# Score products by one Strassen step per pair of token tiles, with two x buffers refilled by GpSimd, in an FNet + PEER kernel

## The chip, the cores and the metric

The kernel runs on one core of one Trainium2 chip. The metric is the device time of one execution in microseconds, as the median of the runs. Before the change it is 764.75 us in three runs (764.59, 764.75 and 765.51).

## The reference

x has 2048 tokens of 640 values. Two branches are mixed by a gate of each token.

```python
# A: FNet.  y = Re(DFT_seq(DFT_hidden(x)))
a = einsum("bsd,ed->bse", x, dft_hid_re);  b = einsum("bsd,ed->bse", x, dft_hid_im)
y = einsum("ts,bse->bte", dft_seq_re, a) - einsum("ts,bse->bte", dft_seq_im, b)
# B: PEER. 32 heads, 2 x 16 keys of 128 values, 256 experts, the best 2 of each head
q = einsum("nd,dhc->nhc", x, w_q)
s1 = einsum("nhd,ed->nhe", q[..., :128], k1);  s2 = einsum("nhd,ed->nhe", q[..., 128:], k2)
# the best 2 of s1 and of s2, their 4 sums, the best 2 of these: top_s, top_e
g = softmax(top_s)
act = gelu(einsum("nd,nhkd->nhk", x, u[top_e]))
out = einsum("nhk,nhk,nhkd->nd", g, act, v[top_e])
gate = sigmoid((x * gate_w).sum(-1))
return gate * y + (1 - gate) * out
```

## The kernel before

All large products are made with operands split in two: a number is rounded to fp32r (h, on ScalarE), the rest l = f - h is taken by a second engine (`split`, L124), and `mm3` (L129) makes three matmuls: h·h, h·l and l·h.

The program goes through 128 **pieces** of the sequence DFT (`seq_piece`, L208). A piece is one of 2 DFT matrices (real, imaginary), 4 column chunks of 512 and 16 tiles of x; it has 15 matmuls of 128x512, which add into PSUM banks 0 to 4. Behind every 16th piece the five banks are copied to the tile ST, VectorE multiplies them by the gates (`gate_piece`), and `store_piece` stores the block P to DRAM (tile pd, five transfers of 256 KB). The x tiles X0 to X15 (h and l of 128x640 each) are made once and stay in SBUF. The DFT matrix comes in piece by piece: loaded by SP five pieces ahead (`load_piece`, tile wf), split three pieces ahead into one of four slots of WS (`split_piece`, L167: h by ScalarE, l by a GpSimd subtraction).

Other work is hung on the pieces by `at(n, f)`: f is emitted behind piece n.

- Pieces 0 to 29: the keys are folded into w_q (`w_part`, L333; w_q comes in 32 transfers of 640 KB, tile wq), which gives a matrix W of 640 x 1024 (32 heads x 2 x 16 keys) in WH and WL; `split_u` prepares u. x transposed comes in per pair of token tiles (`load_xT`, tile xf) and is split into xh and xl (`split_xT`, L370, the l part on GpSimd).
- Pieces 31 to 62: one pair of token tiles per 4 pieces. `score_half` (L429) makes the scores of one tile and one half of the columns, 15 matmuls of 128x512 behind a piece, in banks 5 and 6 by turns; ScalarE copies them to the tile sc. `u_pair` (L576) makes the products with all 256 experts' u for both tiles, 30 matmuls of 128x256 in the same banks, then gelu on ScalarE and two stores, issued by ScalarE.
- VectorE finds the best two of each head (`topk`, L444: maxima, eq, powers, tied) and, after every 4 tiles, the gates (`gates`, L478, with an exp on ScalarE, L500). Later one-hot tables (hot, `experts`) and their products (L668) turn the gates into sums per expert. The order of this work is set by a queue of generators, the **Pump** (L45): TensorE's emitted time gives credit (0.95 of it), and each operation gives back its assumed cost by `yield`. So the costs in the program set where VectorE's work stands among the rest; they are no measured times.
- From piece 128 on, the last stage: 84 steps of two Strassen products with the hidden DFT and v (`step`, L948). DD, the split hidden DFT matrix, is made in pieces from about 66 on (`split_dd`, L709, with GpSimd).

The dependencies between engines are found from the order of the program (semaphores are put in by it); each engine and each DMA queue works its own list in order.

Of the kernel before, what the change touches and what calls it, by code (L numbers as in the profile page):

```python
# [40 lines left out]
AHEAD = 5  # L41
BYPASS = 4

# [51 lines left out]
def gated_mix_kernel(ctx: ExitStack, tc: tile.TileContext, xT, xn, dreT, dimT, wsre, wsim, wq, kT, uT, vv, gw, out):  # L95
# [43 lines left out]
    gdr = dram.tile([2 * S], F32, name="gdr")  # L139
    bg = Pump()  # L140
# [14 lines left out]

    pieces = [(w, c, s) for w in range(2) for c in range(NC) for s in range(NT)]
# [43 lines left out]
    def store_piece(q):  # L200
# [4 lines left out]
        for d in range(KD):  # L205
            eng.dma_start(pd[w, c][d], staged.pop((q, d)))
# [21 lines left out]
    for q in range(2 * NC):  # L228
        n = NT * (q + 1)
        at(n + (2 if q == 0 else -2 if q > 1 else -1), load_row, q)  # L230
        at(n + (7 if q == 0 else 0), gate_piece, q)
        at(n + (8 if q == 0 else 1), store_piece, q)
# [42 lines left out]
    gwb = p1.tile([P, D], F32, name="gwb")  # L275
# [21 lines left out]
    io = p1.tile([P, P], F32)  # L297
# [50 lines left out]
    def split_w(G):  # L348
        c = slice(P * G, P * (G + 1))
        split(wp.pop(G), WH[:, :, c], WL[:, :, c], nc.vector)  # L350
# [3 lines left out]
    def load_u(k):  # L354
        uf[k] = p1.tile([P, NE], F32, name="uf", bufs=2)
        nc.sync.dma_start(uf[k], uT[k])
# [19 lines left out]

    for n in range(NT - 4):
        at(n, load_x, n + 4)
# [7 lines left out]
    for G in range(NG):  # L386
        b = 6 + 3 * G
        for m in range(4 * G, 4 * G + 4):
            at(b, w_part, m)
        at(b, split_w, G)  # L390
        for i, m in enumerate(range(4 * G + WQB, 4 * G + WQB + 4)):
            at(b + i // 2, load_wq, m)
# [7 lines left out]
    at(n - 2, load_xT, 1)  # L400
    N0 = n + 1
# [27 lines left out]
    def score_half(i, a):  # L429
        xh, xl = (xs[t][:, i % 2] for t in ("xh", "xl"))  # L430
        if a == 0:
            while i > 1 and i - 2 not in picked:
                bg.one()
            scs[i] = p2.tile([P, HH, E], F32, name="sc", bufs=2)
        ps = ps_s()
        c = slice(a * TC, (a + 1) * TC)
        for k in range(KD):
            mm3(ps, xh[:, k, :], xl[:, k, :], WH[:, k, c], WL[:, k, c], k == 0, k == KD - 1)
            run_bg(0.68)
        nc.scalar.activation(scs[i].rearrange("p h e -> p (h e)")[:, c], ps, AF.Copy)  # L440
        if a == 1:
            picks(i, scs.pop(i))

    def topk(i, sc):  # L444


        b, ib = divmod(i, NB)
        if ib == 0:
            stats[b] = [p2.tile([P, 2, NB, HH], F32, name=t) for t in ("mm", "tied")]
        mm, tied = stats[b]  # L450
        eq = p2.tile([P, HH, E], F16, name="eq", bufs=1)
        for s in range(2):
            m = mm[:, s, ib, :]
            nc.vector.tensor_reduce(m, sc, op=OP.max, axis=AX.X)  # L454
            yield 1.22
            nc.vector.tensor_tensor(eq, sc, m[:, :, None].to_broadcast([P, HH, E]), op=OP.is_equal)  # L456
            yield 1.31
            if s == 0:
                nc.vector.scalar_tensor_tensor(sc, eq, FAR, sc, op0=OP.mult, op1=OP.add)
                yield 1.44  # L460
            nc.vector.tensor_tensor(eq, eq, powers[:, None, :].to_broadcast([P, HH, E]), op=OP.mult)
            yield 1.0
            nc.vector.tensor_reduce(tied[:, s, ib, :], eq, op=OP.add, axis=AX.X)  # L463
            yield 1.22
# [111 lines left out]
    def u_pair(p):  # L576
        xh, xl = xs["xh"], xs["xl"]
        ps = ps_s((P, 2, 2 * P))
        for n in range(2):
            c = slice(n * P, (n + 1) * P)  # L580
            for k in range(KD):
                mm3(ps[:, n, :], UH[:, k, c], UL[:, k, c], xh[:, :, k, :], xl[:, :, k, :], k == 0, k == KD - 1)
            run_bg(1.8)
        act = p2.tile([P, 2, 2 * P], F32, name="act", bufs=2)
        nc.scalar.activation(act, ps, AF.Gelu_apprx_tanh)
        for n in range(2):
            nc.scalar.dma_start(actd[n][:, 2 * p * P:2 * (p + 1) * P], act[:, n])

    for p in range(NP):
        n = N0 + 4 * p  # L590
        for a in range(4):
            if a == 2:
                at(n + 3, u_pair, p)
                at(n + 3, split_xT, p + 1, 0)
            at(n + 1 + a, score_half, 2 * p + a // 2, a % 2)
        at(n + 4, split_xT, p + 1, 1)
        at(n + 6, load_xT, p + 2)
    N1 = N0 + 4 * NP + 1

# [13 lines left out]
    def experts():  # L613
# [33 lines left out]
        def build(g, c, s):  # L647
# [7 lines left out]
            for o, a, b, op in ((pt, row(0), wt, OP.is_equal), (qt, row(1), wt, OP.is_equal), (pt, pt, row(2), OP.mult)):  # L655
                nc.vector.tensor_tensor(o, a, b, op=op)  # L656
                yield 1.1 + settle()
# [62 lines left out]
    for m in range(KD):  # L720
        for a in range(2):
            at(N1 + 3 + 4 * m + 2 * a, split_dd, m, a)
        at(N1 + 7 + 4 * m, load_dd, m + 2)

# [386 lines left out]
```

## Time and profile before

| what | time |
|---|---|
| median of the runs | 764.75 us (764.59 to 765.51) |
| the profiled execution | 764.93 us |
| its span | 763.2 us |
| TensorE busy | 757.8 us (99%) |
| VectorE busy | 558.7 us (73%) |
| GpSimd busy | 342.6 us (45%) |
| ScalarE busy | 314.4 us (41%) |
| DMA moved | 130.34 MB, mean 171 GB/s |

The span is what the profiler saw of one execution, from its first to its last instruction; 764.93 - 763.2 = 1.7 us lie around it. Engines: PE is TensorE's matmuls, PEld its weight loads (beside the matmuls), DVE VectorE, ACT ScalarE, POOL GpSimd, SP the engine that only issues DMAs; ACTq, SPq are the lists that issue DMAs from an engine. Names such as `sc<-b` are output and input by the program's names, b a PSUM bank. Matmuls are pipelined, so the shown length of one is longer than the distance to the next. L numbers are lines of the program before; in the quoted rows of the changed program, of that one.

### The profile page before, as it was taken

The page shows a single profiled execution, that of the slowest core. Times are in us where ns is not written, and L with a number is a line of the kernel's source. Part 1 is how long each engine was busy: PE and PEld are TensorE (multiplying, and loading weights), DVE is VectorE, ACT ScalarE, POOL GpSimd, SP SyncE. Part 2 cuts the span into 40 slices and gives each one's busy share as a digit, 9 for nine tenths or more (in the row PEclk, how much of TensorE's full clock was granted, in tenths as well). Part 3 has the DMA queues.
Part 4 walks back from the last instruction along what each step waited for, and adds up shares of the span by engine and source line. Part 5 has one row for each costly group of instructions (what it writes and reads, how often), then busy time and mean ns, then how long its engine had stood idle before and what let it go on. Part 6 is the DMA issues. An engine that isn't in the chain of part 4 may idle for free.

```text
span 763.2 us, 11112 instructions
## 1 busy us (share of the span) xinstructions
PE 757.8 (99%) x4091; PEld 620.5 (81%) x4091; DVE 558.7 (73%) x653; ACT 314.4 (41%) x558; POOL 342.6 (45%) x254
## 2 busy tenths in 40 slices
PE   9999999999999999999999999999999999999998
PEld 7777777888888888888888888888888788888886
DVE  6863152566899699999699979669989995357651
ACT  4434123221224442623533784533544653543441
POOL 5533235142242323433148664444357694487252
PEclk9999999999999999999999999999999999999999
DMA  9988695321213322320535342568855659775301
GB/s 335 356 311 314 240 368 210 111 76 42 76 57 79 107 97 64 123 52 21 166 129 168 119 154 72 176 196 289 297 196 193 201 207 368 245 231 175 111 28 70
DMA packets 73398, 130.34 MB, mean 171 GB/s; under 512 B 14848, under 2 KB 22144, under 8 KB 73088
## 3 DMA queue, kind: packets, MB, share of 16 engines
q1 hardware_dynamic: 63040, 113.16, 44.7%
q10 hardware_dynamic: 10304, 16.47, 6.0%
q8 instruction: 32, 0.52, 0.3%
q14 instruction: 22, 0.18, 0.1%
HBM read 102.84 MB, written 25.18 MB: 168 GB/s over the span
## 4 chain that ended last, share of the span: by engine, by line
PE 97%; DVE 1%; POOL 1%; ACT 0%; issue 0%; POOLq 0%
PE b L131 31%; PE b L133 30%; PE b L132 30%; PE b L340 2%; PE b L218 2%; PE b L668 1%; PE b L286 0%; DVE hot L656 0%; DVE vxl L127 0%; POOL WS L127 0%; ACT b L626 0%; DVE tf L760 0%; POOL ts L127 0%; DVE ST L998 0%; ACT WS L126 0%
## 5 line engine op out<-in xcount | busy, mean ns | idle before, releaser
L127 POOL TENSOR_TENSOR WS<-wf,WS 128x512 fp32r<-128x512 f32 x127 | 191.6, 1512 | 254.9 <-ACT WS L126 243.9
L131 PE MATMUL b<-WS,X 128*128 128x512 f32 x620 | 243.2, 392 | 0.0
L132 PE MATMUL b<-WS,X 128*128 128x512 f32 x620 | 241.4, 389 | 0.0
L133 PE MATMUL b<-WS,X 128*128 128x512 f32 x620 | 241.3, 389 | 0.0
L131 PEld LDWEIGHTS b<-WS,X 128*128 128x128 f32 x620 | 116.4, 188 | 28.1 <-issue 3.6
L133 PEld LDWEIGHTS b<-WS,X 128*128 128x128 f32 x620 | 116.4, 188 | 24.3
L132 PEld LDWEIGHTS b<-WS,X 128*128 128x128 f32 x620 | 116.4, 188 | 23.7
L126 ACT ACTIVATE WS<-wf 128x512 fp32r<-128x512 f32 x127 | 79.7, 629 | 103.4 <-PE b L133 50.7
L656 DVE TENSOR_TENSOR hot<-rows,wtab 128x1024 f16<-128x1024 f16 x64 | 64.2, 1026 | 12.6 <-PE b L668 12.6
L454 DVE TENSOR_REDUCE mm<-sc 128x64 f32<-128x1024 f32 x32 | 38.8, 1212 | 41.2 <-ACT sc L440 41.2
L127 POOL TENSOR_TENSOR xl<-xf,xh 128x640 fp32r<-128x640 f32 x16 | 28.9, 1811 | 80.0 <-ACT xh L126 80.0
L440 ACT ACTIVATE sc<-b 128x512 f32<-128x512 f32 x32 | 19.8, 619 | 108.1 <-PE b L133 108.1
L131 PE MATMUL b<-WU,xh 128*128 128x512 f32 x160 | 62.3, 390 | 0.0
L132 PE MATMUL b<-WU,xh 128*128 128x512 f32 x160 | 62.3, 390 | 0.0
L133 PE MATMUL b<-WU,xl 128*128 128x512 f32 x160 | 62.2, 389 | 0.0
L127 POOL TENSOR_TENSOR WS<-ra,WS 128x512 fp32r<-128x512 f32 x39 | 55.3, 1430 | 13.2 <-ACT WS L126 12.9
L126 ACT ACTIVATE WS<-ra 128x512 fp32r<-128x512 f32 x55 | 34.5, 631 | 50.5 <-PE b L133 38.4
L626 ACT ACTIVATE b<-b,mask 128x128 f32<-128x128 f32 x128 | 43.6, 345 | 19.3 <-PE b L668 16.1
L456 DVE TENSOR_TENSOR eq<-sc,mm 128x1024 f16<-128x1024 f32 x32 | 47.6, 1488 | 1.1
L127 POOL TENSOR_TENSOR WP<-ra,WP 128x512 fp32r<-128x512 f32 x18 | 27.8, 1560 | 44.6 <-ACT WP L126 44.5
L196 DVE SCALAR_TENSOR_TENSOR ST<-ST,grow 128x512 f32<-128x512 f32 x40 | 36.3, 970 | 9.2 <-ACT ST L225 9.2
L463 DVE TENSOR_REDUCE tied<-eq 128x64 f32<-128x1024 f16 x32 | 39.0, 1220 | 1.1
(162 smaller groups left out, 1215.5 us busy)
## 6 DMA issues: line engine op xcount, KB each, us to landing
wq<-in_wq SPq DMA_DIRECT2D x32, 640.0 KB, 6.3
wf<-in_wsim SPq DMA_DIRECT2D x64, 256.0 KB, 3.5
wf<-in_wsre SPq DMA_DIRECT2D x63, 256.0 KB, 4.7
ra<-pd SPq DMA_DIRECT2D x47, 256.0 KB, 3.1
pd<-ST ACTq DMA_DIRECT2D x35, 256.0 KB, 3.4
xf<-in_xT SPq DMA_DIRECT2D x16, 320.0 KB, 3.4
ra<-pqs SPq DMA_DIRECT2D x19, 256.0 KB, 5.7
xr<-in_xn SPq DMA_DIRECT2D x15, 320.0 KB, 7.1
```

Source lines behind the costliest of these rows:

```text
L126: nc.scalar.activation(h, f, AF.Copy)
L127: eng.tensor_sub(l, f, h.bitcast(F32))
L131: nc.tensor.matmul(o, wh, ah, start=first, stop=False, skip_group_check=more)
L132: nc.tensor.matmul(o, wh, al, start=False, stop=False, skip_group_check=more)
L133: nc.tensor.matmul(o, wl, ah, start=False, stop=last, skip_group_check=more)
L196: nc.vector.scalar_tensor_tensor(f, f, -1.0 if w else 1.0, g, op0=OP.mult, op1=OP.mult)
L440: nc.scalar.activation(scs[i].rearrange("p h e -> p (h e)")[:, c], ps, AF.Copy)
L454: nc.vector.tensor_reduce(m, sc, op=OP.max, axis=AX.X)
L456: nc.vector.tensor_tensor(eq, sc, m[:, :, None].to_broadcast([P, HH, E]), op=OP.is_equal)
L463: nc.vector.tensor_reduce(tied[:, s, ib, :], eq, op=OP.add, axis=AX.X)
L626: nc.scalar.activation(f[:, :, n], f[:, :, n], AF.Copy, scale=mask4[:, n:n + 1])
L656: nc.vector.tensor_tensor(o, a, b, op=op)
```

## The change

**Scores.** For the k chunks 0 to 3 (of 5) and a pair of tiles, the four products of (two tiles) x (two k halves) with (two k halves) x (two column halves) are made by one Strassen step in Winograd's form: 7 products in place of 8, each of 6 matmuls. With the fifth chunk's 4 x 3 matmuls a pair has 54 matmuls in place of 60. It needs four sums of W (`make_t`: T1 to T4, by VectorE, in pieces 22 to 28, when a column block of W is made) and four sums of x per pair (`sum_xT`: VectorE, then ScalarE rounds and GpSimd subtracts). Products share parts, so ScalarE copies two PSUM banks to another one in each pair, and VectorE adds two partial results from PSUM to sc.

```python
def score_step(p, a):                       # behind pieces n+1 .. n+4 of pair p
    if a == 0:                              # bank 5: A, 6: Y, 7: u, then Z
        products(A, x_part(0, 0, 2) . W11, first=True)
        u_pair(p)
        copy(Z, A)
    elif a == 1:
        products(Z, x_part(0, 2, 4) . W21, x_part(0, 4, 5) . W51)
        copy(sc_half(i0, 0), Z)
        products(Y, s_part(1) . t_part(1), first=True)
        copy(Z, Y)
        load_xT(p + 1)
    elif a == 2:
        products(A, s_part(2) . t_part(2))
        copy(sc_half(i0, 1), A)
        products(Z, s_part(4) . W22, x_part(0, 4, 5) . W52)
        nc.vector.tensor_add(sc_half(i0, 1), sc_half(i0, 1), Z)
        picks(i0, scs.pop(i0))
        products(A, s_part(3) . t_part(3))
        copy(sc_half(i1, 1), A)
        split_xT(p + 1, 0)
    else:
        products(Y, x_part(1, 4, 5) . W52)
        nc.vector.tensor_add(sc_half(i1, 1), sc_half(i1, 1), Y)
        products(A, x_part(1, 2, 4) . t_part(4), x_part(1, 4, 5) . W51)
        copy(sc_half(i1, 0), A)
        picks(i1, scs.pop(i1))
        split_xT(p + 1, 1)
        sum_xT(p + 1)
```

(Shortened: W with row chunk and column half for the slices of WH and WL.) After every second pair one piece has no scores behind it, so the last pair ends at piece 65 in place of 62 (N1 is 66, was 63).

**x tiles.** The sums of W take the buffers X0 to X5. So tiles 0 to 7 are stored to DRAM (xd) once made, and fetched again: while scores are made, through X6 and X7 by turns, issued by GpSimd two pieces (for the first two of a block four) ahead; afterwards back to their own buffers.

```diff
+    def put_x(s):
+        nc.sync.dma_start(xd[s], X[s].bitcast(F32))
+    def get_x(s, tag, eng=nc.gpsimd):
+        X[s] = big.tile([P, 2, D], F32R, name="X", tag=f"X{tag}")
+        eng.dma_start(X[s].bitcast(F32), xd[s])
+    for s in range(AWAY):                   # AWAY = 8
+        at(6 + 2 * s, put_x, s)
+    for s in range(2):
+        at(2 * NT - 5 + s, get_x, s, 6 + s)
...
+    for n in range(2 * NT + 2, NPC):
+        s = n % NT
+        if s < (AWAY if n < N1 - 2 else 4 if n < N1 + 2 else 0):
+            at(n - (2 if s > 1 else 4), get_x, s, 6 + s % 2)
```

**Rest of a DFT piece.** For all pieces 34 to 63 and the even ones from 64 to 90 GpSimd's subtraction becomes an accumulating transfer: ScalarE also writes l = -h, and a DMA issued by GpSimd adds the piece from DRAM to it.

```diff
     def split_piece(n):
         if n < NPC:
-            psp[n] = WS[:, n % 4, 0], WS[:, n % 4, 1]
-            split(pf.pop(n), *psp[n], nc.gpsimd)
+            psp[n] = h, l = WS[:, n % 4, 0], WS[:, n % 4, 1]
+            f = pf.pop(n)
+            if not N0 + 4 <= n < (4 * NT if n % 2 else ACCUM_END):
+                split(f, h, l, nc.gpsimd)
+                return
+            nc.scalar.activation(h, f, AF.Copy)
+            nc.scalar.activation(l, h.bitcast(F32), AF.Copy, scale=-1.0)
+            w, c, s = pieces[n]
+            nc.gpsimd.dma_start(l, (wsre, wsim)[w][c, s], accum_op=OP.add)
```

**Smaller parts.** u's products have a bank of their own (7) and begin it once (start only at n = 0 and k = 0); act has one buffer and is stored by SP. P of q = 1, 2, 3 is stored one chunk behind each of five pieces. The costs in the Pump are 1.27, 1.27, 0.75 and 0.95 in place of 1.31, 1.44, 1.0 and 1.1, and the new VectorE work is charged to it (1.8 for the sums of x, 0.75 for an addition). `split_dd` has a spacing of 5 pieces in place of 4. Some small tiles share buffers (gwb, io, uf).

**Where it moves instructions.** GpSimd at the turn from pair 0 to pair 1 (xl: rest of the transposed x; WS: rest of a DFT piece; tw, h: l parts of the sums of x; X: a fetched tile), before:

```order
L127 TENSOR_TENSOR WS_89<-wf_1346,WS_89 128x512
L127 TENSOR_TENSOR WS_89<-wf_1385,WS_89 128x512
L127 TENSOR_TENSOR xl_1048<-xf_1450,xh_1047 128x640
L127 TENSOR_TENSOR WS_89<-wf_1429,WS_89 128x512
L127 TENSOR_TENSOR xl_1048<-xf_1450,xh_1047 128x640
L127 TENSOR_TENSOR WS_89<-wf_1471,WS_89 128x512
```

and with the change:

```order
L129 TENSOR_TENSOR xl_1108<-xf_1376,xh_1107 128x640
L440 DMA X_1433<-xd_85 128x1280
L181 DMA WS_90<-in_wsre 128x512
L129 TENSOR_TENSOR xl_1108<-xf_1376,xh_1107 128x640
L129 TENSOR_TENSOR tw_921<-xf_1376,tw_925 128x256
L129 TENSOR_TENSOR tw_922<-xf_1376,tw_926 128x256
L129 TENSOR_TENSOR tw_924<-xf_1376,h_1195 128x256
L129 TENSOR_TENSOR tw_923<-xf_1376,h_1195 128x256
L440 DMA X_1489<-xd_85 128x1280
L181 DMA WS_90<-in_wsre 128x512
```

The subtractions for WS are transfers now, the four sums stand behind the second xl, and the fetches X_1433 (used in piece 35) and X_1489 (piece 36) stand between and behind them.

ScalarE at the gates of tiles 4 to 7, in the 51st or 52nd piece (sc: scores; b5, b6, b7: PSUM banks; cc: sums of the candidates, L500 and L627 the exp; pd: the store of P), before:

```order
L440 ACTIVATE sc_2093<-b6_2148 128x512
L126 ACTIVATE WS_89<-wf_2065 128x512
L206 DMA pd02_71<-ST_68 128x512 x5
L500 ACT_TABLE_LOAD
L500 ACTIVATE cc_2212<-cc_2212 128x128
L585 ACT_TABLE_LOAD
```

and with the change:

```order
L534 ACTIVATE sc_2390<-b7_2351 128x512
L534 ACTIVATE b7_2400<-b6_2392 128x512
L178 ACTIVATE WS_90<-wf_2283 128x512
L179 ACTIVATE WS_90<-WS_90 128x512
L217 DMA pd02_71<-ST_68 128x512
L627 ACT_TABLE_LOAD
L627 ACTIVATE cc_2442<-cc_2442 128x128
L534 ACTIVATE sc_2390<-b5_2304 128x512
L534 ACTIVATE sc_2485<-b5_2304 128x512
```

The exp stood behind the score copies and the five stores of P; now two copies out of bank 5 stand behind it, and one store of P at a time between the copies.

More of the change, by code (lines that the diff above doesn't have):

```diff
@@ L41 @@
 AHEAD = 5
+AWAY = 8
 BYPASS = 4
+ACCUM_END = NT * (NC + 2) - 4
 class Pump:
@@ L427, in gated_mix_kernel, with new_sc @@
     picked, rowed = set(), set()
-    def score_half(i, a):
-        xh, xl = (xs[t][:, i % 2] for t in ("xh", "xl"))
-        if a == 0:
[L432 to L442, printed above, removed]
+    def new_sc(i):
+        while i > 1 and i - 2 not in picked:
+            bg.one()
+        scs[i] = p2.tile([P, HH, E], F32, name="sc", bufs=2)
```

143 lines of the change are left out of this document (116 added, 27 removed).

## The prediction

> **What bounds the kernel now.** The page is read first, parts 1 and 4: the busy time of each engine, and the chain that ended last.
>
> ```profile
> span 763.2 us, 11112 instructions
> PE 757.8 (99%) x4091; PEld 620.5 (81%) x4091; DVE 558.7 (73%) x653; ACT 314.4 (41%) x558; POOL 342.6 (45%) x254
> PE 97%; DVE 1%; POOL 1%; ACT 0%; issue 0%; POOLq 0%
> ```
>
> TensorE is busy for 757.8 of 763.2 us and is 97% of the chain. So the time is the sum of its matmuls, and a stall anywhere on it is paid in full. The time line of TensorE around a piece gives the pitch of its matmuls (start, duration, engine, line). The piece whose first matmul starts at 185.32 has 15 of them, and the next score product starts at 188.72.
>
> ```profile
> 180.09 0.28 PE L131 MATMUL b<-xh,WU 128*128 128x256 f32 x1
> ...
> 181.89 0.40 PE L131 MATMUL b<-WU,xh 128*128 128x512 f32 x1
> ...
> 185.09 0.39 PE L133 MATMUL b<-WU,xl 128*128 128x512 f32 x1
> 185.32 0.39 PE L131 MATMUL b<-WS,X 128*128 128x512 f32 x1
> ...
> 188.72 0.39 PE L131 MATMUL b<-WU,xh 128*128 128x512 f32 x1
> ```
>
> A 512-wide matmul costs 3.40 / 15 = 0.227 us (the shown 0.39 overlaps its neighbours), a 256-wide one of the u product 1.80 / 15 = 0.12. A piece is 3.4 us, and u for a pair (30 matmuls) 3.6. Then the table by stretches (span, PE, PEld, DVE, ACT and POOL busy, clock, DMA share, GB/s): two pairs of tiles, and the place where the one-hot products end.
>
> ```profile
> 182.06:212.88 30.82, 30.82 (x151) 26.13 (x151) 23.46 (x37) 9.20 (x14) 9.76 (x6) 1.00 0.18 57
> ...
> 336.16:366.98 30.82, 30.82 (x151) 26.12 (x151) 29.08 (x28) 10.13 (x13) 10.37 (x6) 1.00 0.15 38
> ...
> 589.80:611.19 21.39, 20.28 (x163) 16.63 (x162) 19.85 (x27) 14.24 (x33) 14.89 (x11) 1.00 0.64 195
> ```
>
> While scores are made, TensorE never waits, VectorE is busy for up to 29 of 30.8 us, and GpSimd and the DMA engines are nearly free. Only between 589.8 and 611.2 does TensorE wait 21.39 - 20.28 = 1.1 us.
>
> **What the change removes.** A pair has 54 score matmuls instead of 60, so 8 pairs lose 48 x 0.227 = **10.9 us** of TensorE. The credits of the background queue (VectorE costs now set lower) bring the last one-hot products out by piece 125 instead of after piece 127, away from the crowded end: the 1.1 us should go too (0 to 1.1). Removed: **12.0 us**.
>
> **What it adds on TensorE's path.** Step a of a pair now takes 6 x 0.227 + 3.6 = 5.0, 3.4, 4.8 and 2.7 us (a = 0 to 3), each with a 3.4 us piece ahead. x tiles 0 to 7 no longer stay in SBUF: through two buffers GpSimd fetches the tile of piece n, 640 KB, behind piece n - 2, and its queue is in order. The section on the change shows GpSimd's rows at the turn from pair 0 to pair 1. The WS subtractions became transfers, and X_1433 (piece 35) and X_1489 (piece 36) stand behind copies that can only start when TensorE ends a step. The costs of these copies are in the trace: ScalarE, GpSimd and VectorE at the end of a score half, and then the groups by tile or line (min/median/max ns; the last, ScalarE's, busy us and mean ns).
>
> ```profile
> 185.52 0.60 ACT L440 ACTIVATE sc<-b 128x512 f32<-128x512 f32 x1 [1.15 <-PE b L133]
> 192.32 0.60 ACT L440 ACTIVATE sc<-b 128x512 f32<-128x512 f32 x1 [5.68 <-PE b L133]
> 192.81 0.73 ACT L126 ACTIVATE xh<-xf 128x640 fp32r<-128x640 f32 x1
> 193.62 1.57 POOL L127 TENSOR_TENSOR xl<-xf,xh 128x640 fp32r<-128x640 f32 x1 [5.63 <-ACT xh L126]
> 195.15 2.27 POOL L127 TENSOR_TENSOR WS<-wf,WS 128x512 fp32r<-128x512 f32 x1
> 194.20 2.07 DVE L456 TENSOR_TENSOR eq<-sc,mm 128x1024 f16<-128x1024 f32 x1
> 205.22 0.42 DVE L484 TENSOR_TENSOR tied<-tied,first 128x256 f32<-128x256 f32 x1
> ```
>
> ```profile
> L127 POOL TENSOR_TENSOR WS<-wf,WS x127: 1275/1395/2371, 8.0 to 598.3; 128x512 fp32r<-128x512 f32 x127
> L127 POOL TENSOR_TENSOR xl<-xf,xh x16: 1549/1692/2317, 116.5 to 347.7; 128x640 fp32r<-128x640 f32 x16
> L127 POOL TENSOR_TENSOR ts<-tf,ts x12: 918/922/1277, 566.4 to 621.5; 128x256 fp32r<-128x256 f32 x12
> L456 DVE TENSOR_TENSOR eq<-sc,mm x32: 1217/1226/2628, 146.2 to 389.1; 128x1024 f16<-128x1024 f32 x32
> L461 DVE TENSOR_TENSOR eq<-eq,powers x32: 691/693/1671, 149.2 to 390.3; 128x1024 f16<-128x1024 f16 x32
> ...
> L126 ACT ACTIVATE ts<-tf 128x256 fp32r<-128x256 f32 x18 | 7.1, 414 | 7.4 <-DVE tf L761 4.2 <-DVE tf L762 1.8 <-DVE tf L760 1.4
> ```
>
> From the end of a step: ScalarE starts 0.2 later (185.09 + 0.23 to 185.52), xl starts 1.3 after that (192.32 to 193.62) and takes 1.55 or more, so it ends at 3.1. Behind step 2 the fetch is issued there. Behind step 3, VectorE's first sum of x overwrites what xl reads, and takes 0.42; ScalarE rounds it (0.41); GpSimd's four subtractions take 0.92 each: with 0.05 to 0.1 between them, 3.1 + 0.5 + 0.5 + 3.9 = 8.0. That is the least. In the rows above xl and WS on GpSimd and eq on VectorE make room for each other: eq takes 2.07 against 1.22, WS 2.27 against 1.28. With two VectorE operations (eq, 1.2, and its product with powers, 0.7) pushed in between, the four end at some 10. I take 10.0, and 3.6 behind step 2.
>
> No GpSimd transfer is in the trace. The nearest are SP's loads of the same 640 KB (KB each, median us to landing; then wq's issue in ns and its landing):
>
> ```profile
> wq<-in_wq SPq DMA_DIRECT2D x32, 640.0 KB, 6.3
> dt<-in_vv SPq DMA_DIRECT2D x1, 640.0 KB, 4.3
> L331 SPq DMA_DIRECT2D wq<-in_wq x32: 327/328/1325, 8.8 to 111.2; - x32
> DMA to landing us min/median/max: 3.8/6.3/10.1
> ```
>
> The bounds are 3.8 and 10.1; I take 4.3, a lone load, as the score stretch moves little (38 to 57 GB/s above). Below 3.8 nothing in the trace speaks for it.
>
> - Pieces 35 and 36: X for 36 lands 10.0 + 4.3 = 14.3 after step 3 of pair 0; TensorE is there after a piece and step 0, 3.4 + 5.0 = 8.4. Wait **5.9** in both together (piece 35 takes some 2 of it).
> - Pieces 53 and 54 (pair 4): the same, **5.9**.
> - Piece 39 (behind step 2 of pair 1): 3.6 + 4.3 against a piece and step 3, 6.1: **1.8**.
> - Piece 50: behind step 3 of pair 3 and one accumulating transfer (its issue 0.7, between wq's 0.33 and 1.3): 15.0 against two pieces and step 0, 11.8: **3.2**.
>
> Sum **16.8**. At the least (8.0, 3.1, 0.33 and 3.8) it is 3.4 + 3.4 + 0.8 + 0.3 = 7.9; with 10.5, 4.2, 1.3 and wq's median 6.3 it is 8.4 + 8.4 + 4.4 + 6.3 = 27.5. The Trainium skill, DMA: Bandwidth & Descriptors, "Anatomy of one DMA — SWDGE (gpsimd) path", fits such a transfer as 2.0 us plus its bytes at 436 GB/s. By that a fetch takes an estimated 3.5 us, and the sum would be 3.2 us smaller; no run here shows it yet.
>
> The other wait is ScalarE's. At the gates of tiles 4 to 7 (the second place that the section on the change shows, on ScalarE) the copies that stood ahead of the exp now stand behind it. The exp waits for VectorE's gates, and behind it stands sc_2390<-b5, which must have read bank 5 before step 2 of pair 4 adds its third product to it. How long that takes, from the last operation on a tile's maxima to the copy behind the exp, and VectorE's additions from PSUM:
>
> ```profile
> 203.63 1.22 DVE L463 TENSOR_REDUCE tied<-eq 128x64 f32<-128x1024 f16 x1
> ...
> 208.07 0.29 DVE L499 TENSOR_TENSOR cc<-cc 128x128 f32<-128x128 f32 x1
> ...
> 208.39 0.31 ACT L500 ACTIVATE cc<-cc 128x128 f32<-128x128 f32 x1 [6.85 <-DVE cc L499]
> 208.61 0.58 ACT L440 ACTIVATE sc<-b 128x512 f32<-128x512 f32 x1
> ...
> L922 DVE TENSOR_TENSOR ST<-ST,b x14: 680/687/689, 634.7 to 746.8; 128x512 f32<-128x512 f32 x14
> ```
>
> From 204.85 to the copy's end at 209.2 it is 4.4 us. By the credits these gates begin as piece 51 ends, and TensorE has 15 matmuls, 3.4 us, until that product. The wait is 1.0 plus VectorE's lag. The sums of x and two additions from PSUM (4 x 0.45 + 2 x 0.7) give VectorE 3.2 us more in each pair, against the WS subtractions that no longer push it aside; I take a lag of 0.7: **1.7** (0 if VectorE runs ahead, 4 if it lags by 3). At the other gates the exp stands a piece or more ahead of such a product, and before, nothing hung on that copy.
>
> **What I cost at nothing.** The six copies of a pair on ScalarE (0.6 each, two of them PSUM to PSUM) run beside the 3.4 us of the next piece; without that cover each costs up to 1 us. The sums of W (some 40 operations of 0.42 on VectorE in pieces 22 to 28) lie where VectorE is idle. The eight stores of x, 640 KB each, go to SP's queue among the loads of wq:
>
> ```profile
> 80.00:90.00 10.00, 10.00 (x67) 7.42 (x60) 1.86 (x3) 2.53 (x4) 2.80 (x3) 1.00 0.83 318
> ...
> 54.36 2.29 PE b L340 x32
> ...
> L331 SPq DMA_DIRECT2D wq<-in_wq x2: 382/524/667, 45.2 to 45.6; - x2
> ...
> DMA to landing us min/median/max: 6.8/7.4/8.0
> ...
> wf<-in_wsim SPq DMA_DIRECT2D x64, 256.0 KB, 3.5
> ```
>
> The last of these wq lands at 53.6 and is used in the last quarter of the products from 54.36 on, at 56.1: 2.5 us to spare, against one store of 640 KB ahead of it, 2 us at that row's 318 GB/s. I take 0 (0 to 3). An accumulating transfer of a piece is begun three pieces ahead: beside scores 20 us and more, after piece 66 10.2 us, against two ScalarE operations and a landing like wf's 3.5; taken at 0, its price if late stands below. u's bank begun once is a flag; P stored by chunks, and act stored by SP, take 0.3 to 0.4 us issues off ScalarE's crowded places, worth nothing on TensorE.
>
> **The sum.** The profiled execution took 764.93 us, span 763.2: 764.9 - 12.0 + 16.8 + 1.7 = 771.4. The median of the runs is 0.2 lower, so **771 us**. The bounds: 764.9 - 12.0 + 7.9 = 760.8, and 764.9 - 10.9 + 27.5 + 4 = 785.5.
>
> **The rivals.**
> - *Faster: the fetch is hidden.* The place is pieces 36, 50 and 54; it decides whether X lands within 8.4 us (11.8 for piece 50) of the end of the step. Were GpSimd's chain 4 us shorter than the rows make it and landing 3.8, TensorE would not wait: 764.9 - 12.0 = 752.9 to 754.6 with the exp. For it: WS subtractions no longer stand in GpSimd's queue. Against it: 8.0 is a sum of the shortest rows. Chance 0.25, for all from here up to 761.
> - *The accumulating transfers are late.* From piece 66 to 90 each even piece has 10.2 us: ScalarE's start and two roundings 0.2 + 1.3, an issue of 0.4, so it decides at a landing of 8.3. At wq's longest, 10.1, half of 13 pieces' 1.8 us, as one wait covers the next: 11.7 more, 783. Against it: landings there are near 3.5. Chance 0.08.
> - *The clock falls in the gaps.* Before, the clock granted is 1.00 in every row above, but there is no gap of 4 us in them, and this change makes about three. The Trainium skill, TensorE: Matmul & The Clock Gate, "Why this matters for your kernels", says that a gap of over about 3 us between bursts brings the half clock back. Were TensorE at half its rate for as long as such a gap again (4 us, so 2 us lost), three gaps cost 6: 777. No row before can tell. Chance 0.12.
> - *The forecast*, with its bounds: chance 0.55.
>
> **How the numbers follow.** A measurement of this kernel tells 0.2%, 1.5 us, from no change: faster is below 763.2, slower above 766.3. Of the forecast's 0.55, 0.05 is faster and 0.08 same, at its low end; with the first rival, faster is 0.30, same 0.08, slower 0.62. The range 757 to 785 leaves out most of the first rival (0.15) and little above (0.05).
>
> **What would show it.** TensorE should wait for X from xd at pieces 35, 36, 39, 50, 53 and 54, for some 2, 4, 2, 3, 2 and 4 us; GpSimd's fetch of piece 36 should begin 8 to 10.5 us after step 3 of pair 0. ScalarE's exp should hold bank 5's copy once by 1 to 2 us. The median of eq stays 1.23, and fewer of them come near the 2.63 of now. The 1.1 us near the end should be gone, and the granted clock in the pieces behind the gaps tells the third rival. The forecast is wrong if X lands before the step needs it, or if waits for WS in pieces 66 to 91 make up more than 5 us.

## The result, and the profile after

The changed kernel takes **784.15 us** (median of 4 runs, 783.06 to 788.21) against 765.1 (764.59 to 765.51) before: ratio 1.0259, 95% interval 1.022 to 1.0298. The forecast was 771 within 757 to 785, so the median lies 0.85 us below the top of the range. The profiled execution is the longest of the four, 788.21 us with a span of 786.2, and lies above it; the terms below are those of this execution. First the page: the span, TensorE's line, and the chain that ended last.

```profile
span 786.2 us, 11382 instructions
PE 756.4 (96%) x4043; PEld 615.5 (78%) x4043; DVE 572.2 (73%) x741; ACT 365.8 (47%) x666; POOL 358.7 (46%) x310
...
PE 79%; DMA 6%; DVE 6%; ACT 3%; issue 2%; POOL 2%; ACTq 0%; SPq 0%; DVEq 0%; POOLq 0%
```

There are 48 matmuls fewer (4043, were 4091), which is 10.9 us. But TensorE's busy time fell by 1.4 only, and its idle time rose from 5.4 to 29.8 us; the chain, 97% TensorE before, now goes through DMA, VectorE, ScalarE and GpSimd for 17%. What TensorE waited for (total, times, longest), and where (start of the first matmul behind the wait; pieces 35, 36, 39, 50, 53, 54 and 67, then the one-hot products ahead of piece 125):

```profile
PE b L133 <- DMA X<-xd: 19.6, 8, 8.2
PE b L801 <- DVE cd L765: 3.0, 3, 1.3
PE b L355 <- DMA wq<-in_wq: 1.1, 1, 1.1
...
PE b L134 <- DMA WS<-in_wsim: 0.7, 1, 0.7
...
PE b L133 <- ACT sc L534: 0.3, 1, 0.3
```

```profile
163.42 0.50 PE L133 MATMUL b<-WS,X 128*128 128x512 f32 x1 [2.03 <-DMA X<-xd]
...
174.71 0.50 PE L133 MATMUL b<-WS,X 128*128 128x512 f32 x1 [1.05 <-DMA X<-xd]
...
198.01 0.50 PE L133 MATMUL b<-WS,X 128*128 128x512 f32 x1 [1.91 <-DMA X<-xd]
...
282.99 0.80 PE L133 MATMUL b<-WS,X 128*128 128x512 f32 x1 [8.19 <-DMA X<-xd]
...
307.69 0.50 PE L133 MATMUL b<-WS,X 128*128 128x512 f32 x1 [1.36 <-DMA X<-xd]
...
319.00 0.50 PE L133 MATMUL b<-WS,X 128*128 128x512 f32 x1 [2.67 <-DMA X<-xd]
...
408.30 0.50 PE L133 MATMUL b<-WS,X 128*128 128x512 f32 x1 [2.20 <-DMA X<-xd]
...
620.22 0.44 PE L801 MATMUL b<-hot 128*64 128x64 f16 x16 [1.34 <-DVE cd L765]
621.89 0.64 PE L801 MATMUL b<-hot 128*64 128x64 f16 x16 [1.23 <-DVE cd L765]
```

The six places are those of the forecast, and their sum, 17.2 us, is near its 16.8 (term by term it is not, as the section on the prediction says); piece 67 and a short one at piece 71 add 2.4. Now the stretches behind the gaps (span, PE, PEld, DVE, ACT, POOL, clock, DMA share, GB/s):

```profile
164.29:167.70 3.41, 3.41 (x10) 2.64 (x9) 3.22 (x5) 1.91 (x5) 2.42 (x4) 0.50 0.01 2
198.42:201.83 3.41, 3.41 (x10) 2.64 (x9) 2.71 (x5) 1.33 (x4) 2.42 (x4) 0.50 0.06 11
276.93:287.17 10.24, 4.18 (x10) 3.31 (x11) 10.00 (x11) 3.40 (x5) 2.14 (x3) 0.50 1.03 289
...
621.67:625.08 3.41, 3.19 (x22) 2.65 (x23) 2.83 (x4) 3.31 (x9) 3.33 (x3) 0.50 0.76 255
```

Four times the granted clock is 0.50. In the first row TensorE starts 10 matmuls in 3.41 us where it would start 15. Half of the busy time in the four rows is lost: (3.41 + 3.41 + 4.18 + 3.19) / 2 = 7.1 us. So the account of this execution: 764.9 - 10.9 - 1.1 (the wait of before) + 19.6 + 3.0 + 1.1 + 0.7 + 0.3 + 0.5 (a wait for WS at the start) + 7.1 = 785.2. Of the 3.0 that are left to 788.2, some 0.27 go with each of a dozen gaps, since a matmul ahead of a gap takes its whole 0.39 and not the pitch of 0.227, and the first one behind it 0.50 and not 0.39.

### The profile page after: what moved, and what is told of

The parts are those of the page before. It is cut to its first block, busy times and chain, and to the rows that moved or that the text cites. A ratio compares the mean times of both kernels' runs of the same rounds, so it can differ in the third digit from the quotient of the medians.

```text
span 786.2 us, 11382 instructions
## 1 busy us (share of the span) xinstructions
PE 756.4 (96%) x4043; PEld 615.5 (78%) x4043; DVE 572.2 (73%) x741; ACT 365.8 (47%) x666; POOL 358.7 (46%) x310
## 4 chain that ended last, share of the span: by engine, by line
PE 79%; DMA 6%; DVE 6%; ACT 3%; issue 2%; POOL 2%; ACTq 0%; SPq 0%; DVEq 0%; POOLq 0%
PE b L133 25%; PE b L134 25%; PE b L135 25%; DMA X<-xd 4%; PE b L229 2%; PE b L355 2%; DMA wq<-in_wq 2%; DVE hot L789 1%; POOL tw L129 1%; PE b L801 1%; DVE tf L893 1%; ACT rows L675 1%; ACT b L759 1%; POOL xl L129 1%; DVE ST L207 1%
## 5 line engine op out<-in xcount | busy, mean ns | idle before, releaser
L133 PE MATMUL b<-WS,X 128*128 128x512 f32 x620 | 247.0, 398 | 19.6 <-DMA X<-xd 19.6
L134 PE MATMUL b<-WS,X 128*128 128x512 f32 x620 | 244.2, 394 | 0.7 <-DMA WS<-in_wsim 0.7
L135 PE MATMUL b<-WS,X 128*128 128x512 f32 x620 | 243.7, 393 | 0.0
L129 POOL TENSOR_TENSOR WS<-wf,WS 128x512 fp32r<-128x512 f32 x83 | 125.0, 1512 | 142.1 <-ACT WS L128 137.5
L133 PEld LDWEIGHTS b<-WS,X 128*128 128x128 f32 x620 | 118.1, 190 | 51.1 <-DMA X<-xd 21.7
L135 PEld LDWEIGHTS b<-WS,X 128*128 128x128 f32 x620 | 117.9, 190 | 25.0
L134 PEld LDWEIGHTS b<-WS,X 128*128 128x128 f32 x620 | 118.0, 190 | 24.7 <-DMA WS<-in_wsim 1.1
L789 DVE TENSOR_TENSOR hot<-rows,wtab 128x1024 f16<-128x1024 f16 x64 | 59.7, 960 | 20.1 <-PE b L801 20.1
L129 POOL TENSOR_TENSOR xl<-xf,xh 128x640 fp32r<-128x640 f32 x16 | 27.2, 1704 | 74.1 <-ACT xh L128 74.1
L181 POOL DMA_DIRECT2D WS<-in_wsre x30 | 26.7, 910 | 68.3 <-ACT WS L179 63.0
L583 DVE TENSOR_TENSOR eq<-sc,mm 128x1024 f16<-128x1024 f32 x32 | 43.4, 1355 | 0.9
L207 DVE SCALAR_TENSOR_TENSOR ST<-ST,grow 128x512 f32<-128x512 f32 x40 | 32.7, 874 | 4.6 <-ACT ST L236 4.6
L765 DVE TENSOR_REDUCE cd<-b 128x128 f32<-128x512 f32 x32 | 21.8, 684 | 14.7 <-ACT b L759 9.9
```

Source lines behind the costliest of these rows:

```text
L129: eng.tensor_sub(l, f, h.bitcast(F32))
L133: nc.tensor.matmul(o, wh, ah, start=first, stop=False, skip_group_check=more)
L134: nc.tensor.matmul(o, wh, al, start=False, stop=False, skip_group_check=more)
L135: nc.tensor.matmul(o, wl, ah, start=False, stop=last, skip_group_check=more)
L207: nc.vector.scalar_tensor_tensor(f, f, -1.0 if w else 1.0, g, op0=OP.mult, op1=OP.mult)
```

## The experiments

Theory Q: the fetch of x is late because of its place in GpSimd's queue. Rival L: it is late because its landing is long beside other transfers. Times are medians, beside 765 for the kernel before in the same jobs.

**The fetch ahead of the step.** The loop that registers the fetches stands ahead of that of the score steps.

```diff
+    N1 = N0 + 4 * (NP - 1) + (NP - 1) // 2 + 5
+    for n in range(2 * NT + 2, NPC): ... get_x
     for p in range(NP): ... score_step
-    for n in range(2 * NT + 2, NPC): ... get_x
```

> The fetch of an x tile is put ahead of the score step in the program, so on GpSimd it stands ahead of that step's xl and sums of x. Theory Q (the fetch is late because of what stands ahead of it in GpSimd's queue; alone it lands 4.2 us after its issue): the waits at pieces 35, 36, 39, 53 and 54 (2.0 + 1.1 + 1.9 + 1.4 + 2.7 = 9.0 us) go, and the slices of half clock behind the two of pieces 35 and 39 with them (2 x 1.7): 784.2 - 9.0 - 3.4 = 771.8, say 770 to 773.5. Piece 50 keeps its 8 us, since its fetch still stands behind the sums of x of pair 4, which are one piece earlier in the program. Theory L (the fetch is late because it shares the DMA engines with the accumulating transfers and lands 6 to 12 us after its issue): within 3 us of 784.

778.82 us (777.34 to 779.80). The waits at pieces 35, 36, 39, 53 and 54 are gone and piece 50 keeps 8.1, as Q has it; but 2.6 us came up at piece 37 and 1.2 at piece 55, with a slice of half clock behind the first. GpSimd's rows say why (its fetch for piece 36 at 159.19, for piece 37 at 170.57):

```profile
159.19 0.83 POOL L440 DMA_DIRECT2D X<-xd  x1
162.79 1.56 POOL L129 TENSOR_TENSOR xl<-xf,xh 128x640 fp32r<-128x640 f32 x1 [2.78 <-ACT xh L128]
165.34 1.86 POOL L129 TENSOR_TENSOR tw<-xf,tw 128x256 fp32r<-128x256 f32 x2 [0.99 <-ACT tw L128]
167.20 2.83 POOL L129 TENSOR_TENSOR tw<-xf,h 128x256 fp32r<-128x256 f32 x2
...
170.57 0.87 POOL L440 DMA_DIRECT2D X<-xd  x1
```

One fetch passes the sums of x, and the next one stands behind them. My expectation had removed the waits without asking which fetch is next behind the same chain.

**The fetch on SP**, at its old place in the program.

```diff
-            at(n - (2 if s > 1 else 4), get_x, s, 6 + s % 2)
+            at(n - (2 if s > 1 else 4), get_x, s, 6 + s % 2, nc.sync)
```

> The same fetches, at the same places of the program, issued by SP, whose queue holds no copies. Theory Q: every wait for x goes, that of piece 50 too (19.6 us), and three of the four slices of half clock (1.7 + 1.7 + 2.1): 784.2 - 19.6 - 5.5 = 759, below the kernel before. Theory L: the landings stay at 6 to 12 us and time stays above 775. A third outcome: SP's queue stands still until TensorE has read the old tile, and loads of DFT pieces behind it come late; then waits for WS appear in place of those for X, and the time is 763 to 772.

770.43 us (769.41 to 773.38): 13.7 less, Q's direction, and 11 above its number. The wait at piece 50 is down to 0.2, but x is waited for at pieces 37, 51, 55 and 67 too (7.8 us in all). SP's queue had an in-order chain of its own, the two stores of act, ahead of the fetch for piece 37:

```profile
169.33 0.80 SPq L714 DMA_DIRECT2D actd<-act  x2
170.23 0.40 SPq L440 DMA_DIRECT2D X<-xd  x1
```

**The gaps filled.** 140 matmuls of zeros ahead of five pieces.

```diff
+        for _ in range({35: 16, 39: 16, 50: 70, 54: 20, 67: 18}.get(n, 0)):
+            nc.tensor.matmul(banks[0][:P // 2, :2 * P], zeros, warm, start=False, stop=False, ...)
```

> The changed kernel with 140 extra matmuls of zeros (256 wide, some 0.11 us each) added to a bank ahead of pieces 35, 39, 50, 54 and 67 (16, 16, 70, 20 and 18 of them), in the gaps in which TensorE waits for x; the waits themselves stay. Theory C (TensorE's clock is halved for a slice of 3.41 us behind a slice in which it was idle for more than half): three of the four slices of half clock go, and the kernel gets faster by work that is of no use: 784.2 - 5.5 = 778.7, clock 0.998. Rival (the half clock does not hang on the idle time): 784 to 785.5, clock 0.987 to 0.991 as before.

785.41 us (783.12 to 786.96): no gain, against theory C's number. The clock did rise as C has it, to 0.998, 0.993, 0.995 and 0.998 in the four runs, from 0.987, 0.991, 0.991 and 0.991. In the profiled execution the fillers take 16.5 us of TensorE, waits for x are down from 19.6 to 4.7 (that at piece 36 grew from 1.1 to 2.6), and its 783.1 us are 5.1 below the profiled one of the change; but it is the fastest of its four and the other the slowest. So the clock hangs on the idle time, as C has it; that filling it is worth anything is not shown.

**The fetch ahead, without accumulating transfers** (`split` with GpSimd's subtraction for every piece).

```diff
-            if not N0 + 4 <= n < (4 * NT if n % 2 else ACCUM_END): ...
-            nc.gpsimd.dma_start(l, (wsre, wsim)[w][c, s], accum_op=OP.add)
+            split(f, h, l, nc.gpsimd)
```

> The kernel with the fetch ahead of the step, and with the rest of every DFT piece subtracted on GpSimd again in place of the accumulating transfers. If these transfers cost nothing but what they take from GpSimd, and GpSimd has room for four subtractions of 1.3 to 2.3 us per pair more (23 us of work in 28): the same as the run with the fetch ahead alone, 772 +- 1.5. If they make the landings late (theory L): up to 6 us less. If GpSimd gets too full: its xl and sums come later, waits for the score operands or for WS appear, 774 to 785.

773.15 us (771.37 to 776.27), 5.7 below the run with the fetch ahead alone: L has its share. The wait at piece 50 is 5.7 in place of 8.1, that of piece 37 0.5 in place of 2.6; the two fetches stand at the same places of the queue but land in 5.5 and 5.9 us from their issue in place of 7.5 and 8.6. The half clock takes 6.8 us of the span in place of 17.1, in the fastest execution here against the slowest there (mean granted clocks of 0.990 to 0.995 against 0.988 to 0.991).

**Fetch ahead and on SP.**

> The fetch put ahead of the score step and issued by SP. In the run with SP alone the fetch of piece 37 was issued 6.6 us after its buffer was free, because SP's queue had the store of act ahead of it, and the waits left were 1.8, 2.9, 1.3 and 1.6 us at pieces 37, 51, 55 and 67, with two slices of half clock (3.4). Theory Q (place in the queue): the first three go, with their slices: 770.4 - 6.0 - 3.4 = 761, say 759 to 763, below the kernel before. Theory L (landings of 6 to 12 us beside the accumulating transfers): 767 to 771.

767.89 us (767.11 to 770.17). The waits at pieces 37, 51 and 55 and their slices are gone, as Q has it, though the time lies in L's range. Others have come up that stood in the shadow of these: 2.2 at step 2 of pair 4 for a copy on ScalarE, 2.5 for WS at piece 70 with a slice of half clock, and the 1.7 at piece 67 and the 2.8 of the one-hot products remain.

**Row copies later**, on the changed kernel.

```diff
-            bg.space(lambda a=a: step(a), ... else 8.0)
+            bg.space(lambda a=a: step(a), ... else 28.0 if b == 0 else 8.0)
```

> The changed kernel with the row copies of tiles 0 to 3 (1.97 us each on ScalarE) begun some 20 us later in the program, so that none stands between the end of step 3 of pair 3 and its xh. Theory S (the 8.2 us at piece 50 are 5.0 more than forecast because ScalarE has five copies of ST, 2.5 us, and a row copy, 2.0 us, ahead of xh and of the rounding of the sums): the second xh starts 2.0 us earlier behind that step and the wait at piece 50 falls to some 6.2 us; the waits at 53 and 54 may grow by as much, where the row copies now fall. Rival (the length of the landing alone sets it): 8.2 +- 0.5 us. The time is within 2 us of 784.

783.99 us (two runs, 782.11 and 785.87). ScalarE and GpSimd behind step 3 of pair 3, whose last matmul starts at 262.41, in the changed kernel:

```profile
262.12 2.53 ACT L236 ACTIVATE ST<-b 128x512 f32<-128x512 f32 x5
264.51 1.97 ACT L675 ACTIVATE rows<-rt 128x384 f16<-128x384 f16 x1
...
266.76 0.76 ACT L128 ACTIVATE xh<-xf 128x640 fp32r<-128x640 f32 x1
```

```profile
267.61 1.56 POOL L129 TENSOR_TENSOR xl<-xf,xh 128x640 fp32r<-128x640 f32 x1 [4.10 <-ACT xh L128]
...
275.39 0.90 POOL L440 DMA_DIRECT2D X<-xd  x1
276.77 0.87 POOL L181 DMA_DIRECT2D WS<-in_wsre  x1 [0.49 <-ACT WS L179]
```

and with the row copies later, ScalarE's rows (the step ends at some 259.6) and the wait at piece 50:

```profile
255.95 2.53 ACT L236 ACTIVATE ST<-b 128x512 f32<-128x512 f32 x5
259.76 0.60 ACT L534 ACTIVATE sc<-b 128x512 f32<-128x512 f32 x1 [1.28 <-PE b L135]
260.25 0.73 ACT L128 ACTIVATE xh<-xf 128x640 fp32r<-128x640 f32 x1
```

```profile
276.60 0.80 PE L133 MATMUL b<-WS,X 128*128 128x512 f32 x1 [5.13 <-DMA X<-xd]
```

xh starts 0.7 behind the step, not 4.1 (266.76 - 262.64), and the wait falls by 3.1 to 5.1: theory S, and more of it than expected, since without the row copies ahead the five copies of ST are early too. The landing stays long: 276.60 is 7.75 us from the fetch's issue at 268.85. The time stays within its spread; pieces 53 and 54 wait a little longer (1.5 and 3.1), and two slices of half clock (6.8 us) come there.

**The old credit of the one-hot work**, on the run with the fetch ahead and on SP (`yield 1.1 + settle()` in place of 0.95).

> As the run with the fetch ahead and on SP, with the Pump's cost of a one-hot operation back at 1.1 (0.95 in the change). Theory T1 (the lower cost crowds the tail: two waits of 1.2 us for cd at piece 125 and a slice of half clock, 4 us in all, against one wait of 1.1 before): 3 us below that run. Theory T2 (the one-hot work begins three pieces later since N1 is 66, so it is short of time and a higher cost only makes it later): the same to 4 us above that run.

776.67 us, 8.8 above that run: T2's sign, and twice its size. The tail (the one-hot products around piece 125) has four waits, 10.0 us in all; the longest:

```profile
617.07 0.46 PE L801 MATMUL b<-hot 128*64 128x64 f16 x16 [3.81 <-DVE cd L765]
```

**Fetch ahead and on SP, without accumulating transfers.**

> As the run with the fetch ahead and on SP, with GpSimd's subtractions in place of the accumulating transfers. With GpSimd's fetch ahead, taking these transfers away gave 5.7 us (778.8 to 773.2). If that came through the landings of x alone, which now have time enough: the same as that run within 1.5 us. If the transfers cost something of their own (ScalarE's second rounding, waits for WS in pieces 66 to 90, 1.1 us): 1 to 3 us less, 757 to 760. If GpSimd gets too full: 1 to 5 us more.

766.37 us (765.00 to 770.51), 1.5 below, which does not tell the first theory from the second. The waits for x and WS are down to 0.3; the one behind the exp is now the largest (TensorE, then ScalarE's exp):

```profile
282.38 0.80 PE L133 MATMUL b<-tw,h 128*128 128x512 f32 x1 [4.01 <-ACT sc L528]
```

```profile
281.54 0.31 ACT L621 ACTIVATE cc<-cc 128x128 f32<-128x128 f32 x1 [7.45 <-DVE cc L620]
```

**The exp one step of the Pump later**, on this run: the line with AF.Exp moves from ahead of `yield 1.2` to behind `yield 1.3`.

> As the run with the fetch ahead and on SP and no accumulating transfers, with the exp of the gates emitted one step of the Pump later, behind VectorE's ten small operations that do not need it. In that run TensorE waits 4.0 us in step 2 of pair 4 for the copy of bank 5 that stands behind the exp on ScalarE (idle for 7.5 us until VectorE's gates), and a slice of half clock follows (1.7). Theory X (the exp's place in ScalarE's queue makes this wait): both go, 766.4 - 5.7 = 760.7, say 759.5 to 762.5, below the kernel before. Rival (VectorE itself is late there, and everything behind its lag waits in any order): 764 to 767.

765.38 us (763.75 to 766.49; ratio to before 1.0003, 0.9994 to 1.0013): 1.0 less, not 5.7, so the rival. The wait at pair 4 goes, and one of 3.15 with a slice of half clock comes at step 0 of pair 5. Behind it stands VectorE: the copy waits on ScalarE behind the rounding of the sums of x, and that waits 8.05 us for VectorE's first sum. The rows are ScalarE's, then those of the later half of the score stage (span, PE, PEld, DVE, ... as above):

```profile
295.10 0.42 ACT L128 ACTIVATE tw<-xf 128x256 fp32r<-128x256 f32 x1 [8.05 <-DVE xf L421]
```

```profile
252.80:311.00 58.20, 55.05 (x264) 46.28 (x263) 56.97 (x73) 22.96 (x38) 24.14 (x19) 0.97 0.49 159
311.00:369.00 58.00, 57.49 (x281) 48.36 (x281) 56.59 (x71) 29.80 (x45) 28.09 (x20) 1.00 0.28 92
```

VectorE is busy for 98%. In the kernel before, in two stretches at about the same pieces, it is busy for 58.54 of 61.40 and 52.90 of 62.00 us (95% and 85%).

**A lower credit, 0.85**, on this run.

> The same, with the Pump's cost of a one-hot operation at 0.85 (0.95 in the change, 1.1 before it). At 1.1 the tail got 9 us longer. Theory T2 (the one-hot work is short of time since it begins at piece 66): the two waits of 1.2 to 1.4 us at piece 125 and the slice of half clock behind them (1.6) go: 4 us below the run with the exp later. Rival (VectorE is full there, and a lower cost only makes it lag more behind TensorE): the same to 3 us above it.

766.82 us (764.99 to 768.42), 1.4 above, in the rival's range, though the runs of the two overlap. The two waits ahead of piece 125 do go, and one of 3.3 comes behind piece 86, where VectorE has the one-hot tables too late.

**The exp later, accumulating transfers kept.**

> The run with the fetch ahead and on SP, accumulating transfers kept, with the exp one step later. Theory X: the 2.2 us at step 2 of pair 4 go: 767.9 - 2.2 = 765.7. Against the run with the exp later and without these transfers it tells their own price on the chip: by the waits that the trace of the run with them shows (1.7 for x at piece 67, 2.5 for WS at piece 70, a slice of half clock 1.7) 5 to 6 us; if they are free, less than 1.5.

766.13 us (764.24 to 767.91), 1.8 below the run without the move and 0.7 above that without the transfers; the runs of the two overlap. So in the whole time the transfers cost little. By stages it is otherwise. Here are two stretches, from the first matmul of piece 31 to that of piece 66 (the score stage) and from there to that of piece 127, for the kernel before, the exp later, and the exp later with the transfers:

```profile
130.48:387.24 256.76, 256.76 (x1246) 217.43 (x1245) 209.00 (x231) 91.57 (x126) 79.90 (x49) 1.00 0.27 82
387.24:605.71 218.47, 218.47 (x1397) 179.38 (x1395) 193.96 (x234) 109.95 (x240) 120.85 (x83) 1.00 0.58 185
...
130.64:383.32 252.68, 248.50 (x1198) 209.16 (x1197) 230.70 (x267) 108.06 (x172) 114.40 (x85) 0.99 0.39 127
383.32:609.32 226.00, 221.98 (x1428) 181.04 (x1427) 207.25 (x253) 116.33 (x251) 124.33 (x86) 0.99 0.66 214
...
131.62:379.18 247.56, 246.17 (x1199) 208.34 (x1198) 214.58 (x269) 128.77 (x205) 93.32 (x85) 1.00 0.62 164
379.18:608.55 229.37, 224.07 (x1429) 181.87 (x1428) 195.60 (x250) 122.93 (x262) 114.75 (x86) 0.99 0.71 224
```

With the transfers the score stage is 9.2 us shorter than before, most of the 10.9; without them it is 4.1 shorter. VectorE is busy in it for 214.6 us with them and for 230.7 without. The other two runs that differ by the transfers alone agree: 248.4 us with them (fetch ahead and on SP) and 253.3 without. Behind piece 66 it turns round: the stretch is 10.9 us longer than before with the transfers, with waits of 2.2 for x, 0.7 for WS and 2.4 for the one-hot products and two slices of half clock, and 7.5 longer without them. (Some 2 us of this is work that the kernel before has behind piece 127.) All this is from one profiled execution of each.

**Sums of x on GpSimd**, on the run with the exp later and no accumulating transfers.

```diff
-            nc.vector.tensor_add(a22, a21, a22)        # and the three subtractions
-            bg.credit -= 1.8
+            nc.gpsimd.tensor_add(a22, a21, a22)
```

> As the run with the exp later, with the four sums of x of each pair made by GpSimd in place of VectorE, and their 1.8 no longer charged to the Pump. In that run VectorE is busy for 58.3 of 59.8, 57.0 of 58.2 and 56.6 of 58.0 us in the last three quarters of the score stage, and TensorE waits 3.2 us at step 0 of pair 5 for a ScalarE copy that stands behind the rounding of the sums, whose sums stand behind VectorE's backlog; a slice of half clock follows. Theory V (VectorE is the bound of the score stage once TensorE has 10.9 us less): VectorE gets 8 x 1.8 = 14 us of room, and the 3.2 + 0.5 + 0.5 us and the slice (1.7) go: 765.4 - 5.9 = 759.5, say 758 to 762. Rival (GpSimd's sums take twice as long, 0.92 against 0.43 us, stand ahead of the splits that the next step needs, and hold up VectorE beside them as in the rows of before): 764 to 768.

**763.26 us** (761.90 to 765.40) beside 764.74: ratio 0.9983, interval 0.9973 to 0.9992, so 0.2% below the kernel before. It is the lowest of all, 2.1 below the run it starts from, not 5.9, and between the ranges of theory and rival. VectorE is nearly as full as ever, here over the same pieces 31 to 66:

```profile
131.96:382.65 250.69, 247.81 (x1199) 209.48 (x1198) 224.95 (x242) 107.28 (x172) 151.02 (x113) 0.99 0.40 130
```

With 242 operations in place of 267 it is busy for 224.95 us in place of 230.70. One group shows where the rest goes: eq times powers in the score stage (131 to 369 us; count, busy, mean ns), before, changed, exp later, and sums on GpSimd:

```profile
L461 DVE TENSOR_TENSOR eq<-eq,powers 128x1024 f16<-128x1024 f16 x29 | 24.9, 860 | 1.1
```

```profile
L588 DVE TENSOR_TENSOR eq<-eq,powers 128x1024 f16<-128x1024 f16 x24 | 18.3, 762 | 0.8
```

```profile
L582 DVE TENSOR_TENSOR eq<-eq,powers 128x1024 f16<-128x1024 f16 x26 | 26.5, 1020 | 0.9
```

```profile
L581 DVE TENSOR_TENSOR eq<-eq,powers 128x1024 f16<-128x1024 f16 x27 | 33.8, 1252 | 1.0
```

The same operation takes 0.76 us where GpSimd's subtractions have become transfers, and 1.25 where GpSimd does most. What stands beside it makes the difference: in these four stretches the operation took 0.68 to 0.70 us each of the 51 times that no tensor operation of GpSimd ran at the same time, and 1.24 in the mean, up to 1.98, the 55 times that one did. So of 14 us given to VectorE, 0.23 x 27 = 6 went back in this group. (Other groups moved less or the other way: eq<-sc,mm takes 1.51 in the mean of the run with the exp later and 1.41 here.)

## Why the prediction was right, and where it was not

- **Removed, 10.9 us: right.** In the run with the exp later, pieces 31 to 34 with the steps of pair 0 take 29.5 us against 30.8 before: 1.3 per pair, 6 x 0.227.
- **Removed, 1.1 us at the end: wrong.** 3.0 us of waits and 1.6 of half clock came in its place. I took the lower credit alone and left out that the one-hot work begins three pieces later (N1 is 66). With the old credit the run with the fetch ahead and on SP takes 8.8 us more: the lower credit was needed to hold the tail, it was not a gain.
- **Fetches behind step 3, 5.9 twice: the mechanism right, the sizes less.** The fetch of piece 36 is issued 8.7 us behind the step (169.96 - 161.24, its last matmul at 161.01; the row follows), in the range of 8.0 to 10.5 (the two VectorE operations that I put between the sums come behind them), and lands 4.7 from its start (4.3 taken). That gives 13.4 against 8.4, but TensorE needs it 1.7 later because of the half clock that the wait at piece 35 itself set off: 3.3, measured 2.0 + 1.1.

```profile
169.96 0.60 POOL L440 DMA_DIRECT2D X<-xd  x1
```

  For piece 54 the issue comes at some 7.7, below the least that I gave, and the wait is 4.0.
- **Piece 39, 1.8: right** (1.9). **Piece 50, 3.2: this term was mis-sized** (8.2, beyond the 6.3 of its upper bound). The fetch is issued 12.75 behind the step, not 10.7, because at the end of a DFT block five copies of ST and a row copy stand ahead of xh on ScalarE (the row copies moved: 3.1 less); and it lands 7.6 from its start, not 4.3, among two accumulating transfers and another fetch (without them, a wait of 5.7 where 8.1 was). "A lone load" was the wrong row for it: the landings of GpSimd's fetches have a median of 6.3, and this kind reaches 12.8 (last section).
- **The exp, 1.7: nothing in this kernel.** TensorE does not wait at step 2 of pair 4; the 0.3 for a ScalarE copy above is at 260.46, in step 3 of pair 3. In the runs where the long wait at piece 50 is gone, the exp costs 2.2 and 4.0, so the mechanism is right; that this wait hid it is argued, not tested.
- **The wq behind the stores of x: 1.1**, in the 0 to 3 that I gave.
- **The clock, a rival at 0.12 with 6 us: it happened, on top of the forecast, at 7.1 us.** The price was near; that it needs gaps of 4 us was wrong, 2 us do. For the profiled execution the forecast is made up by 771.4 + 7.1 (clock) + 2.8 (x, 19.6 in place of 16.8) + 3.0 (tail) + 2.3 (wq, WS and the start) + 3.0 (ends of gaps) - 1.4 (ScalarE's copies, 0.3 in place of 1.7) = 788.2.
- **How much of it was luck.** The direction and the path were right: TensorE waits for x at the six places, by GpSimd's queue. The sum of these places is near by luck: -2.8 (pieces 35 and 36), -1.9 (53 and 54), +0.1 (39) and +5.0 (50). The top of the range was made of longer chains and landings (27.5 us of waits for x, 4 for the exp); they came to 19.6 and nothing, and the half clock and the tail, which are in no bound, filled the rest.
- **The rival "the fetch is hidden", 752.9 to 754.6: settled against, and its number too.** With the fetch hidden, all but piece 67's, the kernel takes 763 to 768 and not 754, because behind each wait stood the next. VectorE's 3.2 us more per pair were in the working, and "busy for up to 29 of 30.8" was quoted; but as the pair gets shorter by 1.4 these two fill VectorE, and no rival said so. Where GpSimd subtracts beside it, most of the gain is gone in the stage itself: it is 4.1 us shorter and not 10.9, with TensorE's longest wait there behind VectorE's late sums. Where the transfers are kept, it is 9.2 shorter, and the gain is lost behind piece 66. So the 10.9 us have no one place: VectorE's backlog is shown for the first kind of run alone, by the contrast with the second; the one attempt to relieve VectorE left it nearly as full.

What stays open: what the last waits of the run with sums on GpSimd hang on (2.9 us behind piece 60 for a ScalarE copy, a slice of half clock behind it, 2.7 in the tail), and what the stores of x cost by themselves in the first stage. Transfers up to piece 63 and subtractions from there on, with the exp later, would join the shorter halves: by the rows above an estimated 131.6 + 247.6 + 381.4 (the exp later, from piece 66 to the end) = 760.6 us of span, against 764.7 and 763.9 in the two runs. No run tried any of these.

## What to carry to other kernels

Work taken off the engine on the path is worth only what the next engine has free in the same stage: set its busy time, with the change's additions, against the stage's new length, and make it a rival if it comes near. That room hangs on the neighbours too: VectorE's work of the score stage took 214.6 us beside transfers and 230.7 beside GpSimd's subtractions. When a transfer moves to a compute engine's in-order queue, ask of each fetch what stands ahead of it, of the next one too; an early place on a queue without such copies was worth 16 us here. And price a wait of TensorE of 2 us or more with the half clock behind it.

## What the runs showed of the hardware

- **The half clock comes in slices of 3.41 us on a fixed grid**: the slow stretches above begin 10, 33 and 134 slices after the first, and last one or three. In the traces of the change and of all twelve experiments there are 27 falls ahead of the last matmul, each behind a slice in which TensorE was idle for 1.64 us or more; no slice idle for 1.9 or more was without one, and the longest idle time without one was 1.86. Between 1.64 and 1.86 it went both ways. So a gap of 1.91 us that lies within one slice was enough (piece 39), and one of 2.67 us that falls on two (1.6 and 1.1, piece 54) was not; here are those two:

```profile
314.47:317.89 3.42, 1.86 (x16) 1.65 (x14) 3.35 (x4) 2.26 (x4) 1.50 (x3) 1.00 0.85 204
317.89:321.30 3.41, 2.30 (x10) 1.92 (x11) 3.31 (x4) 0.85 (x2) 0.87 (x1) 1.00 1.05 321
```

  The Trainium skill, TensorE: Matmul & The Clock Gate, "What's actually happening", has a free-running window of 3413 ns; the trace agrees (3.41). It puts the fall behind an idle window; here windows idle for about half did it, and the measurement decides.
- **VectorE's operations with two SBUF inputs pay for GpSimd's work**: 0.76 to 1.25 us in the mean for the same operation, above, and 0.68 to 0.70 wherever no GpSimd tensor operation ran beside it, while a reduction with one input stays at 1.21 in all four. The Trainium skill, SBUF — State Buffer, "SBUF: two separate sides", says that the two engines share a pair of ports that one holds for a whole instruction; the rows agree in direction.
- **Landings of 640 KB fetches depend on company**: GpSimd's take 4.2 to 5.3 us from the start of their issue where no other of its transfers is under way ahead of them, and up to 12.8 beside another fetch and accumulating transfers. Here are the least, the median and the longest of its 24:

```profile
DMA to landing us min/median/max: 4.2/6.3/12.8
```

  The fit of the Trainium skill that the prediction cites makes an estimated 3.5 us of it; the trace has 4.2 at the least and 6.3, nearly twice the 3.5, in the median, so the measurement decides.
